# First token pair of a two-layer MLP behind attention: w_out's product turned, one float32 quad, cheaper sign handling

## The chip, the cores and the metric

One NeuronCore of a Trainium2 chip runs the whole program. Its engines are TensorE (PE in the profile, with its weight loads listed as PEld), VectorE (DVE), ScalarE (ACT), GpSimd (POOL) and SyncE (SP), whose queue issues the DMAs. The metric is the device time of one execution in microseconds; lower is better.

## The reference

Linear attention over 4 batches, 8 heads, 576 positions, head size 64, then two MLPs over 2,304 tokens with d_model 512 and d_ff 2,048. The activations are float32; the MLP weights arrive as float64.

```python
q_s = softmax(q, axis=-1); k_s = softmax(k, axis=2)
kv = np.einsum('bhsd,bhse->bhde', k_s, v)
attn = np.einsum('bhsd,bhde->bhse', q_s, kv)          # -> x [2304, 512]
h = x @ w_in;  g = maximum(h, 0) + log1p(exp(-abs(h)));  x = g @ w_out       # layer 0, softplus
h = x @ w_in2; g = where(h > 0, h, exp(minimum(h, 0)) - 1); out = g @ w_out2 # layer 1, ELU
```

## The kernel before

**Tiling.** The 2,304 tokens are six blocks of 384, taken in three pairs p = 0, 1, 2. The 2,048 hidden features are eight quads f = 0 to 7 of 256. The program runs layer m = 0 over the three pairs, then layer m = 1; inside a pair, quad after quad, "up" (h = w_in^T x, hidden features on the partitions), the activation g, and "down" (w_out's product). The down product of a quad stands beside the up product of the next one.

**Up.** A quad goes up by seven products over 2 x 2 blocks instead of eight (`add_up`, L833). Each operand is split into a rounded part and a rest (fp32r), so a product is six matmuls of 384 columns. `add_forms` makes the seven forms of x for a pair (`ts` L614, `xf` L603 and L607; forms 1 and 2 need the pair's first block only), `add_w_in` the seven forms of the weights (`st` L726, `wf` L742 and L746). The results are added up in PSUM and on DVE (`s` L846, `h` L867).

**Down.** g is split into `gh` (ACT, L969) and `gl` (DVE, L973), w_out likewise into the halves of `wo` (L766, L770). In pair 0 of layer 0 a step of `add_down` (L1045) has g as the stationary operand and 512 output features as columns, so the result has tokens on the partitions. In pairs 1 and 2 of layer 0 the product is *turned* (`add_down_turned`, L1007): w_out is stationary, the 768 tokens of the pair are the columns, in a matmul of 512 and one of 256, and output features lie on the partitions. Turned results are stored feature by feature, and layer 1 loads them as they are (`add_y`); those of pair 0 are stored by tokens, loaded again and transposed on PE (`py`, L566, 24 of them) with a copy on ACT (`sx`, L577).

**Direct quads.** Quads 0 and 1 of pair 0 take another way, since the opening has little time to prepare operands: float32 matmuls on x and the unsplit weights (`add_up_direct`, L895; down at L1040). Each float32 matmul stands as two records in the trace.

**Weights.** `add_words` turns float64 to float32 by integer operations on the two 32-bit words: ACT scales the high word (L662), DVE shifts it left (L666), DVE puts the sign back by and-or (L670, SCALAR_TENSOR_TENSOR), ACT scales the low word (L676), DVE adds (L687, a custom operation; ISA in the order). There are 32 such conversions, through two `raw` buffers.

**Attention** of a block is made just ahead of its pair: key maxima (`mx`, `pt`, `m`, `pb`), exponentials, `pk` (L390) and `kvbd`; for the queries `qm`, `qd`, `qn`, `pq` (L506), `px` (L522), and the copy into `sx` (L535). Block t = 1 belongs to pair 0 as well. The exponential and softplus need different function tables in ACT, so ACT_TABLE_LOAD stands between them.

**Order.** `Plan.order` lists every step with an estimated duration, buffers and due times, and at each turn gives an engine the ready step that is latest by its due time. `PRI` (L1344) shifts the due times of the attention steps, of the first pair's weights (i0 to i7, o0 to o7) and of others. Every engine then runs its own list in order.

Of the kernel before, what the change touches and what calls it, by code (L numbers as in the profile page):

```python
# [20 lines left out]
class Plan:  # L21
# [37 lines left out]
    def order(self):  # L59
# [23 lines left out]
        seq = []  # L83
        while len(seq) < n:
# [79 lines left out]
def attention_moe_moe_kernel(  # L164
# [97 lines left out]
    direct = lambda m, p, f: (m, p) == (0, 0) and f < 2  # L262
# [372 lines left out]
    def add_words(m, s, f, ring="ti"):  # L635
# [24 lines left out]
        @step(ACT, t_act(n), w=[rk])  # L660
        def _():
            nc.scalar.activation(hi(), hi(), AF.Copy, scale=2.0**-112)  # L662
# [350 lines left out]
    def add_down(m, p, f):  # L1013

        wk = ("wo", m, "o", f) if p == direct(m, 0, f) else ("wo", m, "o", f, p)
        t0 = after_quad(m, p, f)
        if turned(m, p):
            return add_down_turned(m, p, f, wk, t0)
# [4 lines left out]
        for (i, j, r), at in zip(order, fill):  # L1023
            j, half = at_(m, p, f, i, j)
            col = at_(m, p, f, j, half)[1] * BLK + r * P
# [3 lines left out]
            whole = direct(m, p, f)  # L1029
            gk, w32 = ("g", m, p, f, i), ("w", "ti", m, "o", f)  # L1030

            @step(
                PE, 0.86 if whole else DN, w=[] if first else [ak],
                r=[gk, w32] if whole else [hk, lk, ("woh", m, f), ("wol", m, f)], hold=[] if whole else [wk],
                make=[(ak, f"acc{half}")] if first else [], due=t0 + at + 0.01, line=("acc", half, r),
            )
            def _(col=col, j=j, hk=hk, lk=lk, ak=ak, first=first, whole=whole, gk=gk, w32=w32):
                ps = new(ak) if first else T[ak]
                if whole:
                    nc.tensor.matmul(  # L1040
                        ps, T[gk][:, col : col + P], T[w32][:, j * DM : (j + 1) * DM], start=first, stop=False,
                    )
                    return
# [241 lines left out]
    def add_store(m, p):  # L1285
# [180 lines left out]
```

## Time and profile before

| | us |
|---|---|
| three timed runs, median (range) | 833.11 (832.82 to 833.67) |
| profiled execution: its own time | 833.62 |
| its span, first to last instruction | 831.9 |
| PE busy | 809.3 |
| DVE busy | 657.5 |
| ACT busy | 564.7 |

The granted TensorE clock was full (0.998 over the span). PE's busy time is the union of matmul records, whose ends are modelled and overlap the next start; the distance between two starts tells what a matmul costs in a stream. Idle time of an engine counts only where the engine that sets the end waits for it.

### The profile page before, as it was taken

The page shows a single profiled execution, that of the slowest core. Times are in us where ns is not written, and L with a number is a line of the kernel's source. Part 1 is how long each engine was busy: PE and PEld are TensorE (multiplying, and loading weights), DVE is VectorE, ACT ScalarE, POOL GpSimd, SP SyncE. Part 2 cuts the span into 40 slices and gives each one's busy share as a digit, 9 for nine tenths or more (in the row PEclk, how much of TensorE's full clock was granted, in tenths as well). Part 3 has the DMA queues.
Part 4 walks back from the last instruction along what each step waited for, and adds up shares of the span by engine and source line. Part 5 has one row for each costly group of instructions (what it writes and reads, how often), then busy time and mean ns, then how long its engine had stood idle before and what let it go on. Part 6 is the DMA issues. An engine that isn't in the chain of part 4 may idle for free.

```text
span 831.9 us, 13270 instructions
## 1 busy us (share of the span) xinstructions
PE 809.3 (97%) x5110; PEld 732.4 (88%) x5110; DVE 657.5 (79%) x1088; ACT 564.7 (68%) x889; POOL 6.1 (1%) x28
## 2 busy tenths in 40 slices
PE   5799999999999999999999999999999999999997
PEld 4455788888889999999999998898999999999997
DVE  7879999979887768777679788968468697766775
ACT  4878987876787856756657767667466675557552
POOL 2000000000000000000000000000000000000000
PEclk9999999999999999999999999999999999999999
DMA  9597786636985556576855898987687676787563
GB/s 288 155 284 234 225 283 197 196 115 206 284 263 215 181 206 236 206 253 221 321 191 218 289 371 331 328 325 242 239 311 292 234 284 222 271 278 301 202 225 147
DMA packets 75166, 205.33 MB, mean 247 GB/s; under 512 B 18784, under 2 KB 34144, under 8 KB 65632
## 3 DMA queue, kind: packets, MB, share of 16 engines
q1 hardware_dynamic: 75104, 204.49, 71.0%
q8 instruction: 40, 0.66, 0.3%
q14 instruction: 22, 0.18, 0.1%
HBM read 143.65 MB, written 60.82 MB: 246 GB/s over the span
## 4 chain that ended last, share of the span: by engine, by line
PE 82%; DVE 8%; ACT 5%; DMA 2%; issue 2%; DVEq 0%; ACTq 0%; SPq 0%
PE ub L833 21%; PE acc L1007 15%; PE acc L1045 13%; PE uc L833 11%; PE Pb L1185 8%; PE ua L833 5%; PE Pc L1185 4%; PE Pa L1185 2%; PE px L522 1%; DMA wf_i<-wfd 1%; DVE mt L346 1%; PE acc L1040 1%; PE pk L390 1%; DMA raw_i<-in_moe_w_in_dram 1%; PE pq L506 1%
## 5 line engine op out<-in xcount | busy, mean ns | idle before, releaser
L833 PE MATMUL ub<-xf,wf_i 128*128 128x384 f32 x1104 | 226.5, 339 | 1.4 <-ACT s L846 1.1
L833 PEld LDWEIGHTS ub<-xf,wf_i 128*128 128x128 f32 x1104 | 189.3, 188 | 13.4 <-ACT s L846 4.3
L846 ACT COPY s<-ub 128x384 f32<-128x384 f32 x138 | 65.8, 477 | 72.7 <-PE ub L833 71.6
L833 PE MATMUL uc<-xf,wf_i 128*128 128x384 f32 x552 | 111.8, 337 | 0.7 <-ACT g L916 0.7
L1007 PE MATMUL acc<-gh,wo_o 128*128 128x512 f32 (+1 forms) x512 | 111.7, 340 | 0.0
L1045 PE MATMUL acc<-wo_o,gh 128*128 128x512 f32 x336 | 106.7, 398 | 0.0
L833 PEld LDWEIGHTS uc<-xf,wf_i 128*128 128x128 f32 x552 | 95.1, 188 | 5.7 <-ACT g L916 1.9
L867 DVE TENSOR_TENSOR h<-uc,s 128x384 f32<-128x384 f32 x92 | 51.1, 555 | 52.6 <-PE uc L833 47.5
L1007 PEld LDWEIGHTS acc<-gh,wo_o 128*128 128x128 f32 x512 | 82.9, 188 | 7.3
L1045 PEld LDWEIGHTS acc<-wo_o,gh 128*128 128x128 f32 x336 | 61.4, 188 | 9.0 <-ACT yt L1295 0.2
L1045 PE MATMUL acc<-wo_o,gl 128*128 128x512 f32 x168 | 66.5, 396 | 0.0
L1007 PE MATMUL acc<-gl,wo_o 128*128 128x512 f32 (+1 forms) x256 | 65.5, 336 | 0.0
L973 DVE TENSOR_TENSOR gl<-g,gh 128x768 fp32r<-128x768 f32 x60 | 57.2, 953 | 8.4 <-ACT gh L969 8.3
L833 PE MATMUL ua<-xf,wf_i 128*128 128x384 f32 x276 | 56.0, 337 | 0.0
L969 ACT CAST gh<-g 128x768 fp32r<-128x768 f32 x60 | 50.2, 836 | 7.1 <-DVE g L960 6.3
L833 PEld LDWEIGHTS ua<-xf,wf_i 128*128 128x128 f32 x276 | 47.9, 188 | 1.4 <-ACT sx L535 0.3
L746 DVE TENSOR_TENSOR wf_i<-st_i,wf_i 128x1024 fp32r<-128x1024 f32 x30 | 36.7, 1222 | 15.1 <-ACT wf_i L742 15.1
L1007 PEld LDWEIGHTS acc<-gl,wo_o 128*128 128x128 f32 x256 | 39.1, 188 | 5.3
L916 ACT ACTIVATE g<-h 128x384 f32<-128x384 f32 (+1 forms) x44 | 30.2, 686 | 16.3 <-DVE h L867 16.1
L1045 PEld LDWEIGHTS acc<-wo_o,gl 128*128 128x128 f32 x168 | 31.5, 187 | 6.8
L742 ACT CAST wf_i<-r_i 128x512 fp32r<-128x512 f32 (+1 forms) x48 | 23.2, 511 | 16.5 <-PE uc L833 16.4
L742 ACT CAST wf_i<-st_i 128x1024 fp32r<-128x1024 f32 x30 | 31.4, 1048 | 1.1 <-DVE st_i L726 1.0
(282 smaller groups left out, 1429.2 us busy)
## 6 DMA issues: line engine op xcount, KB each, us to landing
wf_i<-wfd SPq DMA_DIRECT2D x16, 1792.0 KB, 8.2
ws<-wos SPq DMA_DIRECT2D x28, 1024.0 KB, 5.4
raw_i<-in_moe_w_in_dram SPq DMA_DIRECT2D x16, 1024.0 KB, 6.5
raw_o<-in_moe_w_out_dram SPq DMA_DIRECT2D x16, 1024.0 KB, 7.4
wo_o<-wod SPq DMA_DIRECT2D x14, 1024.0 KB, 5.5
wfd<-wf_i SPq DMA_DIRECT2D x8, 1792.0 KB, 7.8
r_i<-w32i SPq DMA_DIRECT2D x24, 512.0 KB, 6.0
wod<-wo_o SPq DMA_DIRECT2D x8, 1024.0 KB, 5.2
```

What stands on the lines that cost most here:

```text
L346: top = lambda o, x, y: nc.vector.tensor_tensor(o, x, y, op=ALU.max)
L742: nc.scalar.copy(view(0, lo, n, c), get())
L746: nc.vector.tensor_tensor(view(1, lo, n, c), get(), view(0, lo, n, c).bitcast(F32), op=ALU.subtract)
L833: nc.tensor.matmul(ps[:, :BLK], T[wk][:, lo : lo + P], T[xk][:, (2 * c + kc) * BLK : (2 * c + kc + 1) * BLK], start=(i in first and kc == ...
L846: nc.scalar.copy(new(sk), T[key][:, :BLK])
L867: nc.vector.tensor_tensor(T[hk][:, half * BLK : (half + 1) * BLK], T[key][:, :BLK], T[sk], op=ALU.add)
L916: nc.scalar.activation(o, i, AF.Softplus)
L969: nc.scalar.copy(new(hk), T[gk])
L973: nc.vector.tensor_tensor(new(lk), T[gk], T[hk].bitcast(F32), op=ALU.subtract)
L1007: nc.tensor.matmul(ps, T[wk][:, lo : lo + P], T[g][:, cols], start=(first and n == 0 and starts), stop=(f == NQ - 1 and j == 1 and n == 2) ...
L1045: nc.tensor.matmul(ps, T[g][:, col : col + P], T[wk][:, (2 * a + j) * DM : (2 * a + j + 1) * DM], start=(first and n == 0), stop=(f == NQ ...
L1185: nc.tensor.matmul(ps[:, x * 256 : x * 256 + 256], T[fk][a][:, r * P : (r + 1) * P], T[ck][:, q * 512 + b * 256 : q * 512 + b * 256 + 256] ...
```

## The change

Four edits, and new numbers in `PRI`. (1) `direct` holds for quad 0 alone; quad 1 of pair 0 goes by seven products and split operands like quads 2 to 7. (2) `turned` holds for all pairs of layer 0, so pair 0 is stored by features, and layer 1 loads it without transposes. (3) Quad 0's down product is turned too, by a new function with float32 matmuls: block 0 as 384 columns, block 1 as 128 and 256. (4) Where the planner has exp's table loaded at the scaling of a high word, ACT scales by a Prelu in place of a copy: for negative numbers its slope -2^32 clears the sign and sets a bit that the shift by three moves into the sign's place, so the and-or is left out. Six of the 32 conversions go this way, five of them in pair 0, both of quad 0 among these.

```diff
+            if i in self.either and table == "exp":
+                gone.add(self.either[i][0])
+                self.light.add(self.either[i][1])
...
-    direct = lambda m, p, f: (m, p) == (0, 0) and f < 2
+    direct = lambda m, p, f: (m, p) == (0, 0) and f < 1
...
+            if tk in plan.light:
+                nc.scalar.activation(hi(), hi(), AF.Prelu, scale=2.0**-112, alpha=-(2.0**32))
+            else:
+                nc.scalar.activation(hi(), hi(), AF.Copy, scale=2.0**-112)
...
-            nc.vector.scalar_tensor_tensor(
-                T[tk], words(1), 0x80000000, T[tk], op0=ALU.bitwise_and, op1=ALU.bitwise_or
-            )
+            if tk not in plan.light:
+                nc.vector.scalar_tensor_tensor(
+                    T[tk], words(1), 0x80000000, T[tk], op0=ALU.bitwise_and, op1=ALU.bitwise_or
+                )
...
-    turned = lambda m, p: m == 0 and p > 0
+    turned = lambda m, p: m == 0
+
+    def add_down_direct(f):
...
+        for n, (t, j, kc) in enumerate((t, j, kc) for t in range(2) for j in range(2) for kc in range(KC)):
...
+                lhs = T[w32][:, j * DM + kc * P : j * DM + kc * P + P]
+                g = T[gk][:, j * BLK : (j + 1) * BLK]
+                ps = T[keys[0]]
+                if not t:
+                    nc.tensor.matmul(ps[:, :BLK], lhs, g, start=first, stop=False, skip_group_check=True)
+                    return
+                more = T[keys[1]][:, kc % 2 * 256 : kc % 2 * 256 + 256]
+                nc.tensor.matmul(ps[:, BLK:], lhs, g[:, :P], start=False, stop=False, skip_group_check=True)
+                nc.tensor.matmul(more, lhs, g[:, P:], start=first and kc % 2 == 0, stop=False, skip_group_check=True)
...
-        k00=97, q00=38, k01=54, q01=13, k02=167, q02=154, k03=94, q03=54, k10=9, q10=83, k12=24, q12=11,
...
+        k00=52.5, q00=663.5, k01=151, q01=397.5, k02=204, q02=426, k03=1516, q03=209.5, k10=55, q10=109, k12=155.5,
```

Lines move by up to 32: L607 is now L613, L614 L620, L670 L682, L687 L701, L833 L847, L895 L909, L973 L987, L1007 L1046; the new direct down product is L1014 to L1018.

DVE, the first conversion (of quad 0's w_in, `raw_i` to `w_ti_i`). Before:

```order
L666 TENSOR_SCALAR ti_i_509<-raw_i_404 128x1024
L403 RECIPROCAL rs_2_507<-rs_2_507 128x2
L491 TENSOR_TENSOR qn_2_518<-q_2_387,qd_2_500 128x2x3x64 x2
L670 SCALAR_TENSOR_TENSOR ti_i_509<-raw_i_404,ti_i_509 128x1024
L687 ISA w_ti_i_545<-raw_i_404,ti_i_509 128x2048
L607 TENSOR_TENSOR xf_0_1_550<-sx_0_175,xf_0_1_550 128x768
```

Now:

```order
L677 TENSOR_SCALAR ti_i_488<-raw_i_344 128x1024
L477 TENSOR_REDUCE qd_0_494<-q_0_414 128x6
L352 TENSOR_TENSOR mt_0_503<-k_0_442 128x512
L352 TENSOR_TENSOR mt_0_503<-mt_0_503 128x2x128
L352 TENSOR_TENSOR mt_0_503<-mt_0_503 128x2x64
L352 TENSOR_TENSOR mx_0_507<-mt_0_503,k_0_442 128x128
L482 TENSOR_SCALAR qd_0_494<-qd_0_494 128x6
L487 RECIPROCAL qd_0_494<-qd_0_494 128x6
L497 TENSOR_TENSOR q_0_414<-q_0_414,qd_0_494 128x2x3x64
L405 TENSOR_SCALAR rs_0_548<-pk_0_518 128x1
L701 ISA w_ti_i_550<-raw_i_344,ti_i_488 128x2048
```

Between the shift and the final addition the and-or L670 is gone, and steps of the query and key chains of blocks 0 and 1 stand there.

PE, the opening, from a direct product of the pair's first block to the `px` matmuls that give block 1's x for the first four heads. Before (`up_0_0_671` and `up_0_1_703` are quad 1's):

```order
L1040 MATMUL acc_0_0_2_609<-w_ti_o_592,g_0_0_0_588 128x512
L390 MATMUL pk_0_624<-v_0_525,k_0_526 64x65 x36
L895 MATMUL up_0_0_671<-sx_0_175,w_ti_i_665 128x384 x4
L506 MATMUL pq_0_694<-ident,qn_0_676 128x128 x3
L506 MATMUL pq_1_699<-ident,qn_0_676 128x128 x3
L895 MATMUL up_0_1_703<-sx_0_175,w_ti_i_665 128x384 x4
L522 MATMUL px_0_716<-xq_0_693,kvbd_0_148 128x3x64
L522 MATMUL px_0_716<-xq_0_693,kvbd_0_152 128x3x64
```

Now (`up_0_0_585` and `up_0_1_646` are quad 0's):

```order
L909 MATMUL up_0_0_585<-sx_0_175,w_ti_i_550 128x384 x4
L396 MATMUL pk_0_598<-v_0_441,k_0_442 64x65 x36
L909 MATMUL up_0_1_646<-sx_0_175,w_ti_i_550 128x384 x4
L512 MATMUL pq_0_671<-ident,qn_0_658 128x128 x3
L512 MATMUL pq_1_676<-ident,qn_0_658 128x128 x3
L1014 MATMUL acc_0_0_682<-g_0_0_0_644,w_ti_o_635 128x384
L528 MATMUL px_0_686<-xq_0_670,kvbd_0_148 128x3x64
L528 MATMUL px_0_686<-xq_0_670,kvbd_0_152 128x3x64
L528 MATMUL px_1_689<-xq_1_675,kvbd_1_149 128x3x64
L528 MATMUL px_1_689<-xq_1_675,kvbd_1_153 128x3x64
```

Quad 1's up product and all but one of the down steps of block 0 no longer stand ahead of these `px` matmuls.

DVE, where the forms of x that need both blocks begin (`ts_0_1`). Before:

```order
L670 SCALAR_TENSOR_TENSOR ti_o_689<-raw_o_611,ti_o_689 128x1024
L687 ISA w_ti_o_709<-raw_o_611,ti_o_689 128x2048
L614 TENSOR_TENSOR ts_0_1_731<-sx_1_174,sx_0_175 128x768
L666 TENSOR_SCALAR ti_i_739<-raw_i_680 128x1024
L614 TENSOR_TENSOR ts_0_2_741<-sx_1_174,ts_0_1_731 128x768
L670 SCALAR_TENSOR_TENSOR ti_i_739<-raw_i_680,ti_i_739 128x1024
L607 TENSOR_TENSOR xf_0_6_744<-ts_0_2_741,xf_0_6_744 128x768
L687 ISA ti_i_739<-raw_i_680,ti_i_739 128x2048
L607 TENSOR_TENSOR xf_0_5_754<-ts_0_1_731,xf_0_5_754 128x768
```

Now (`ti_i_663`, `st_i_0_692`, `wf_i_0_697` are quad 1's w_in):

```order
L740 TENSOR_TENSOR st_i_0_692<-st_i_0_692,ti_i_663 128x256
L760 TENSOR_TENSOR wf_i_0_697<-ti_i_663,wf_i_0_697 128x512
L740 TENSOR_TENSOR st_i_0_692<-ti_i_663 128x256
L760 TENSOR_TENSOR wf_i_0_697<-ti_i_663,wf_i_0_697 128x256
L740 TENSOR_TENSOR st_i_0_692<-ti_i_663,st_i_0_692 128x256
L620 TENSOR_TENSOR ts_0_1_718<-sx_1_176,sx_0_175 128x768
L677 TENSOR_SCALAR ti_o_721<-raw_o_654 128x1024
L620 TENSOR_TENSOR ts_0_2_724<-sx_1_176,ts_0_1_718 128x768
L682 SCALAR_TENSOR_TENSOR ti_o_721<-raw_o_654,ti_o_721 128x1024
L760 TENSOR_TENSOR wf_i_0_697<-st_i_0_692,wf_i_0_697 128x1024
L701 ISA ti_o_721<-raw_o_654,ti_o_721 128x2048
```

Two direct quads' conversions stood ahead of `ts_0_1`; now quad 1's forms of w_in do, and the and-or and rounding of the next weights stand between `ts_0_2` and the first form.

## Rows read from the trace of the kernel before

**Rows 1.** The page: span, busy time (sections 1 and 2).
```profile
PE 809.3 (97%) x5110; PEld 732.4 (88%) x5110; DVE 657.5 (79%) x1088; ACT 564.7 (68%) x889; POOL 6.1 (1%) x28
...
DVE  7879999979887768777679788968468697766775
```

**Rows 2.** Four stretches: us, busy us of each engine (instructions), clock, DMA, GB/s.
```profile
0.00:58.00 58.00, 43.03 (x413) 28.62 (x414) 46.31 (x105) 37.18 (x59) 5.71 (x25) 0.97 0.81 235
58.00:112.00 54.00, 53.61 (x276) 38.00 (x275) 53.56 (x81) 46.21 (x62) 0.13 (x1) 1.00 0.80 258
112.00:200.00 88.00, 87.66 (x493) 74.62 (x492) 78.98 (x121) 71.69 (x108) 0.13 (x1) 1.00 0.54 177
```

**Rows 3.** Timeline of PE: start us, us, engine, line, tiles, shape, xcount [idle before].
```profile
67.25 2.74 PE L895 MATMUL up<-sx,w_ti_i 128*128 128x384 f32 x8
69.83 1.02 PE L1040 MATMUL acc<-w_ti_o,g 128*128 128x512 f32 x2
...
109.09 0.62 PE L1045 MATMUL acc<-wo_o,gh 128*128 128x512 f32 x2
...
109.78 1.20 PE L833 MATMUL ub<-xf,wf_i 128*128 128x384 f32 x6
...
262.93 1.20 PE L833 MATMUL ub<-xf,wf_i 128*128 128x384 f32 x6
263.97 0.86 PE L1007 MATMUL acc<-gh,wo_o 128*128 128x512 f32 x4
264.67 0.51 PE L1007 MATMUL acc<-gl,wo_o 128*128 128x512 f32 x2
265.01 1.20 PE L833 MATMUL uc<-xf,wf_i 128*128 128x384 f32 x6
```

**Rows 4.** A group of PE, whole run: xcount | busy us, mean ns | idle before.
```profile
L566 PE MATMUL py<-ident,yl 128*128 128x128 f32 x24 | 3.6, 272 | 0.0
```

**Rows 5.** Groups of DVE from 57 to 190 us, by shape.
```profile
L973 DVE TENSOR_TENSOR gl<-g,gh 128x768 fp32r<-128x768 f32 x12 | 11.4, 954 | 0.3 <-ACT gh L969 0.3
L746 DVE TENSOR_TENSOR wf_i<-st_i,wf_i 128x1024 fp32r<-128x1024 f32 x8 | 9.8, 1223 | 1.7 <-ACT wf_i L742 1.7
L770 DVE TENSOR_TENSOR wo_o<-ti_o,wo_o 128x1024 fp32r<-128x1024 f32 x6 | 7.3, 1220 | 0.1
...
L670 DVE SCALAR_TENSOR_TENSOR ti_i<-raw_i,ti_i 128x1024 uint32<-128x1024 uint32 x6 | 7.3, 1210 | 0.0
L867 DVE TENSOR_TENSOR h<-uc,s 128x384 f32<-128x384 f32 x12 | 6.6, 554 | 1.2 <-PE uc L833 1.1
L726 DVE TENSOR_TENSOR st_i<-ti_i 128x256 f32<-128x256 f32 x12 | 5.0, 420 | 0.0
```

**Rows 6.** Groups of ACT, whole run, by shape.
```profile
L662 ACT ACTIVATE raw_o<-raw_o 128x1024 f32<-128x1024 f32 x16 | 18.4, 1152 | 0.4 <-DMA raw_o<-in_moe_w_out_dram 0.2
...
L916 ACT ACT_TABLE_LOAD x11 | 14.1, 1283 | 0.2
...
L381 ACT ACTIVATE k<-k 128x1152 f32<-128x1152 f32 x6 | 7.0, 1168 | 0.8 <-DVE k L373 0.7
```

**Rows 7.** Timelines of DVE, then PE, about 112 us.
```profile
111.09 1.22 DVE L746 TENSOR_TENSOR wf_i<-st_i,wf_i 128x1024 fp32r<-128x1024 f32 x1
...
112.57 1.22 PE L833 MATMUL ub<-xf,wf_i 128*128 128x384 f32 x6
```

**Rows 8.** Waits of DVE up to 60 us: us in total, times, longest.
```profile
DVE mt L346 <- DMA k<-in_k_dram: 3.7, 1, 3.7
...
DVE k L373 <- PE pb L366: 1.5, 1, 1.5
DVE qd L471 <- ACT q L467: 1.0, 1, 1.0
```

**Rows 9.** Timelines about the second block: PE, then DVE.
```profile
55.63 1.46 PE L522 MATMUL px<-xq,kvbd 128*128 128x192 f32 x8
...
57.72 0.96 DVE L614 TENSOR_TENSOR ts<-sx,sx 128x768 f32<-128x768 f32 x1 [2.60 <-ACT sx L535]
```

More of the change, by code (lines that the diff above doesn't have):

```diff
@@ L34, in __init__ @@
         self.maker, self.gives, self.place = {}, {}, {}
+        self.either, self.light = {}, set()
     def add(self, eng, dur, fn, r=(), w=(), new=(), due=None, after=0.0, behind=(), port=False, hold=(), tab=None):
@@ L82, in order @@
         lock, table = 0.0, "exp"
-        seq = []
+        seq, gone = [], set()
         while len(seq) < n:
@@ L116, in order @@
                 dur *= PE_EARLY
+            if i in gone:
+                dur = 0.0
+            if i in self.either and table == "exp":
+                gone.add(self.either[i][0])
+                self.light.add(self.either[i][1])
             table = self.tab[i] or table
@@ L661, in _ @@
         def _():
-            nc.scalar.activation(hi(), hi(), AF.Copy, scale=2.0**-112)
+            if tk in plan.light:
+                nc.scalar.activation(hi(), hi(), AF.Prelu, scale=2.0**-112, alpha=-(2.0**32))
+            else:
+                nc.scalar.activation(hi(), hi(), AF.Copy, scale=2.0**-112)
+        scaled = _
         @step(DVE, t_dve(n, True), r=[rk], make=[(tk, "ti")], line="ti")
@@ L973, in _ @@
             nc.vector.tensor_tensor(new(lk), T[gk], T[hk].bitcast(F32), op=ALU.subtract)
-    at_ = lambda m, p, f, j, half: (half, j) if direct(m, p, f) else (j, half)
-    turned = lambda m, p: m == 0 and p > 0
+    turned = lambda m, p: m == 0
+    def add_down_direct(f):
+        t0 = after_quad(0, 0, f)
+        pace = (7 * UP + 4 * R * DN) / (4 * KC)
+        for n, (t, j, kc) in enumerate((t, j, kc) for t in range(2) for j in range(2) for kc in range(KC)):
+            gk, w32 = ("g", 0, 0, f, t), ("w", "ti", 0, "o", f)
+            keys = [("acc", 0, 0, kc)] + [("acc", 0, 0, KC + kc // 2)] * t
+            first = f == 0 and j == 0
+            made = [keys[t]] if first and not (t and kc % 2) else []
+            @step(
+                PE, 0.65, w=[key for key in keys if key not in made], r=[gk, w32],
+                make=[(key, f"acc{kc // 2}") for key in made], due=t0 + n * pace + 0.01, line=("acc", kc),
+            )
+            def _(t=t, j=j, kc=kc, gk=gk, w32=w32, keys=keys, made=made, first=first):
+                for key in made:
+                    new(key)
+                lhs = T[w32][:, j * DM + kc * P : j * DM + kc * P + P]
[7 more added lines that the diff above has]
+                nc.tensor.matmul(more, lhs, g[:, P:], start=first and kc % 2 == 0, stop=False, skip_group_check=True)
     def add_down_turned(m, p, f, wk, t0):
@@ L1016, in add_down @@
         t0 = after_quad(m, p, f)
+        if direct(m, p, f):
+            return add_down_direct(f)
         if turned(m, p):
@@ L1023, in add_down, with _ @@
         for (i, j, r), at in zip(order, fill):
-            j, half = at_(m, p, f, i, j)
-            col = at_(m, p, f, j, half)[1] * BLK + r * P
+            j, half = i, j
+            col = half * BLK + r * P
             hk, lk, ak = ("gh", m, p, f, i), ("gl", m, p, f, i), ("acc", m, p, half, r)
             first = f == 0 and j == 0
-            whole = direct(m, p, f)
-            gk, w32 = ("g", m, p, f, i), ("w", "ti", m, "o", f)
             @step(
-                PE, 0.86 if whole else DN, w=[] if first else [ak],
-                r=[gk, w32] if whole else [hk, lk, ("woh", m, f), ("wol", m, f)], hold=[] if whole else [wk],
+                PE, DN, w=[] if first else [ak], r=[hk, lk, ("woh", m, f), ("wol", m, f)], hold=[wk],
                 make=[(ak, f"acc{half}")] if first else [], due=t0 + at + 0.01, line=("acc", half, r),
             )
-            def _(col=col, j=j, hk=hk, lk=lk, ak=ak, first=first, whole=whole, gk=gk, w32=w32):
+            def _(col=col, j=j, hk=hk, lk=lk, ak=ak, first=first):
                 ps = new(ak) if first else T[ak]
[L1039 to L1043, printed above, removed]
                 for n, (g, a) in enumerate(((hk, 0), (hk, 1), (lk, 0))):
```

7 lines of the change are left out of this document (4 added, 3 removed).

## The prediction

> **What bounds the kernel now.** I read the page's busy shares first. TensorE (PE) is busy 97% of the span and VectorE (DVE) 79%, but the slices of DVE show nines in the opening quarter and fours to eights behind it [rows 1]. So I cut the run by stage. Up to 58 us PE is busy 43.0 of 58 us. From 58 to 112 us PE and DVE are both full, 53.61 and 53.56 of 54 us; from 112 to 200 us PE is full and DVE has 9 us of room [rows 2]. The kernel is therefore PE's instruction stream, started late by the opening, and in the first pair of token blocks DVE keeps up only just.
>
> "Busy" overstates matmuls, because their recorded times overlap, so I price PE by start-to-start distances. Four float32 matmuls of 384 columns (eight records, two for each) go from 67.25 to 69.83 us: 0.645 us each. Six rounded (fp32r) matmuls of 384 columns go from 262.93 to 263.97: 0.174 us each. Three of 512 columns go from 109.09 to 109.78: 0.23 us each. One turned step, three of 512 and three of 256, goes from 263.97 to 265.01: 1.04 us [rows 3]. With these, and the small attention matmuls priced in the same way, PE's rows add up to 795 us of work. The remaining 37 us of the span are the start (5 us until the first matmul), the stores at the end (5 us) and 26 us in which PE is held up, some 17 of them before 50 us.
>
> **The change part by part: PE.** (a) Hidden quad 1 of the first pair goes up by seven products instead of directly. Removed: 16 float32 matmuls at 0.645 = 10.3 us. Added: 7 x 6 at 0.174 = 7.3 us. -3.0 us. (b) Its down product: removed 12 float32 matmuls of 512 columns; by columns from the row of 384, 0.645 x 512/384 = 0.86 each, 10.3 us; added eight turned steps at 1.04 = 8.3 us. -2.0 us. (c) Quad 0's direct down product is turned too: 8 of 384, 8 of 128 and 8 of 256 columns in place of 12 of 512. Both are 6,144 columns, 10.3 us. Zero. (d) Quads 2 to 7: twelve steps of three 512-column matmuls (12 x 0.69 = 8.3 us) become eight turned steps (8.3 us). Zero, though it is 12 instructions more for each quad. (e) The first pair's output now lies in DRAM with features in rows, so the 24 transposes L566 before the second layer go. They are at most their 3.6 us [rows 4]; at 0.645/2 x 128/384 = 0.108 us for a single-record matmul of 128 columns, 2.6 us; I take something between that and nothing hidden, 2.3 us. Sum: **-7.3 us of PE work**, and PE is the engine that sets the end from 58 us on, so all of it counts if PE can be fed as early as now. Nothing hides it.
>
> What speaks against (b) and (d) is the shorter matmul: each one has its own weight load, and the seven turned quads have 84 more of them. In the trace the turned step's 1.04 us is its columns at the pace of the 512-column rows (3 x 0.23 + 3 x 0.117), so the loads behind 256 columns are covered [rows 3], and I take zero. Uncovered they would cost 732.4 / 5110 = 0.143 us each [rows 1], 12.0 us, which is rival 3. The Trainium skill, "TensorE: Matmul & The Clock Gate" (LDWEIGHTS, and Back-to-back issue gap), says that a 128-column load takes about 107 ns however many rows it has, and that in a real stream of pairs the spacing is set by load and matmul together. By that rule an estimated 9 us of loads would come into the open; the trace's 1.04 us does not agree.
>
> **DVE and ScalarE (ACT) in the first pair.** Quad 1's new way adds on DVE, at the means of [rows 5] less 0.08 us by which neighbours overlap: four sums of its weights 1.35, three roundings 2.1 (1.14 for 1,024 columns, the rest by columns), three additions h 1.4, two gl 1.75, and the rounding of w_out 1.14, which so far is done in pair 1. Together 7.7 us. Removed: six and-ors (L670) of the 32, five of them in the first pair, 5 x 1.14 = 5.7 us. Net +2.0 us for DVE in a stretch where it has no room, while PE loses 5.0 us there. This is the part that can eat the gain, and I cost it by a balance.
>
> The balance: for each handover, DVE's work queued ahead of it (all rows of its order at the means of their groups) minus PE's work ahead of its use. That difference plus DVE's idle time until then is how far PE must lag. Before, the tightest handover is quad 4's rounded weights: DVE's 185 rows sum to 99.15 us, its row ends at 112.31, so DVE had idled 13.2 us; PE's work ahead is 89.2 us; the lag is 10.0 + 13.2, and PE takes these weights at 112.57, 0.26 us after they are ready [rows 7]. So the sum reproduces the trace. In the order of the changed kernel the tightest handovers are quad 3's rounded weights (80.6 - 66.2 = 14.4 us) and the key maximum of pair 1 (146.8 - 131.3 = 15.4 us). The lag at PE stays what it was if DVE idles 15.4 - 10.0 = 5.4 us less than now.
>
> Does it? Of the 13.2 us, 3.7 are the first key's load, 1.5 the wait L373 on a matmul queued behind a down product, 1.0 the wait on an exponential [rows 8], 2.6 the wait of ts L614 for the second block's x [rows 9]; the rest is short gaps. The second block's x is the key. Before, its last matmuls end at 57.1 us [rows 9], behind 34.9 us of PE work, quad 1's direct up product among it. Now 25.2 us stand ahead of them, so they end near 57.1 - 9.7 = 47.4, ACT's copies near 48, and DVE, with 42.0 us of work ahead of ts, reaches it at 42.0 + 3.7 + some 2.5 = 48.2: no wait. The matmul behind the wait of 1.5 now stands ahead of every down product. I take 8 us of idle: 3.7, 1.0, some 3.3 of short gaps. Bounds: 5.5 (hardly a gap) and 13.2 (as now). With 8, the lag is 15.4 + 8 = 23.4 against 23.2: +0.3 us.
>
> The multiplication that stands in for the and-or (a Prelu) has no row. Its bounds are a copy-with-scale of 1,024 columns, 1.15 us, and an exponential of 1,152, 1.17 us [rows 6]: the same pace, so I take 1.15 and no cost. (The Trainium skill, "ScalarE: Activation LUTs", What ACT_TABLE_LOAD costs, gives every function the same pace; for a Prelu no run here shows it yet.) ACT gains 4.8 us of work in the first pair (three copies s, casts of weights and of g) and loses four of 23 table loads, 4 x 1.28 = 5.1 us [rows 6]; it has 7.8 us of room from 58 to 112 us [rows 2], so both are hidden there; if ACT lost that room, 4.8 us would be the price.
>
> SP's queue: twelve stores and loads of 256 KB around the old transposes become six stores and two loads; they lie some 200 us after their writers and hide. At the pair's end the same six accumulators are copied out through the same two buffers. In the opening the raw weights still have two buffers, so the third raw load waits for the first conversion, as now; behind it in ACT's order stand the copies of the second block.
>
> **The sum**, against the profiled execution, 833.62 us (its span 831.9; the median of the three timed runs, 833.11, is 0.5 lower): 833.6 - 7.3 + 0.3 = **826.6 us**.
>
> **Rivals.** (1) *DVE idles as now.* The new order keeps 13.2 us of idle, because every handover is tighter: lag 15.4 + 13.2 = 28.6, 5.4 more than now; 833.6 - 7.3 + 5.4 = 831.7, no difference that a measurement shows. For it: both engines now wait for each other from 58 to 150 us, so short waits add up. Against: two named waits go. Idle of 10 to 13 us lies between and gives 828.5 to 831.4. (2) *The second block is late*, the slower side. If the third raw load lands late, ACT stands at it with the copies of the second block behind it, and ts cannot start. Every microsecond by which ts starts after 48.2 + (13.2 - 8) = 53.4 us adds to the 831.7; from 56.5 us on the kernel is slower by over 0.2% (834.8), and with ts at 57.7 as before it takes 836.0. For it: ts did start at 57.72 in the old order [rows 9]. Against: 9.7 us of PE work have gone from ahead of it. (3) *Weight loads in the open*: 833.6 - 7.3 + 12.0 = 838.3 us. For it: more and shorter matmuls in all eight quads; against: the turned steps of pairs 1 and 2 show the loads covered. (4) The change does not do what it says: excluded for the work, since the built order shows the instructions gone.
>
> **How the numbers follow.** Chance 0.66 for the forecast (822.5 to 829.5: idle 5.5 gives 824.1, and small waits elsewhere move 1.5 either way), 0.10 for 829.5 to 831.4, 0.02 for less than 822.5, 0.11 for rival 1 and its neighbourhood (831.4 to 834.8), 0.09 for rival 2, 0.02 for rival 3. The range 822.5 to 832.0 leaves out under 2 in 10. A measurement of this kernel can tell about 0.2%, 1.7 us: faster means under 831.4, slower over 834.8. So faster 0.78, same 0.11, slower 0.11.
>
> **What would show it.** In the changed profile: 24 transposes L566 gone and L1046 at 1.04 us a step; quad 0 alone in float32; ts of the first pair starting near 48 us (rival 1: near 53; rival 2: after 56); DVE full from there to some 150 us with PE's waits on DVE under 3 us in total. Wrong would be: PE waiting on gl, h or rounded weights from 50 to 150 us for 5 us or more, turned steps of the first pair longer than 1.1 us, or an unchanged time with all this in place, which would put a new wait behind 200 us, where I assumed none.

## The result, and the profile after

The changed kernel takes 825.21 us (median of seven runs, 824.13 to 829.62) against 833.29 for the kernel before beside it: ratio 0.9914, 95% interval 0.9899 to 0.9928. The forecast was 826.6, and 826.33 is what the profiled execution took. Five more runs in another comparison gave 825.79, ratio 0.9917 (0.9905 to 0.9929).

The page of the changed kernel, its busy shares and VectorE's (DVE) slices, answers to [rows 1]:

```profile
PE 803.3 (97%) x5216; PEld 744.6 (90%) x5216; DVE 656.0 (80%) x1094; ACT 559.7 (68%) x886; POOL 6.3 (1%) x28
...
DVE  7899999968988767777779688877468697767674
```

106 matmul records more, yet TensorE (PE) is busy 6 us less. The same three stretches as in [rows 2] (us, busy us of PE, its loads, DVE, ACT and POOL, clock, DMA, GB/s):

```profile
0.00:58.00 58.00, 42.88 (x411) 31.10 (x412) 48.05 (x111) 37.99 (x62) 5.57 (x25) 0.97 0.86 244
58.00:112.00 54.00, 54.00 (x302) 48.72 (x301) 53.69 (x80) 45.10 (x63) 0.00 (x0) 1.00 0.73 236
112.00:200.00 88.00, 87.64 (x617) 79.07 (x616) 79.01 (x126) 72.74 (x109) 0.56 (x2) 1.00 0.62 202
```

DVE is full from 58 to 112 us, as before, and PE now is to the last hundredth. PE's waits from 50 to 200 us shrink from four lines, 0.9 us in all, to one (waited for: us, times, longest):

```profile
PE ua L847 <- ACT kvbd L422: 0.4, 1, 0.4
```

I price PE's stream as the prediction did: every record at the pace of its shape (start to start), and what its starts are later than that I call *held up*. So "PE work" is a count of instructions times paces of the trace; that the paces hold is seen where the held-up time of a full stretch stays near zero. "Median" is that of all runs of the kernel in its comparison, "profiled" the traced execution to which the rest belongs; all in us.

| kernel | median | profiled | PE work | held up | before 50 | 50 to 150 | 150 to 250 | later |
|---|---|---|---|---|---|---|---|---|
| before | 833.3 | 833.6 | 795.95 | 25.9 | 16.7 | 1.7 | 4.1 | 3.4 |
| changed | 825.2 | 826.3 | 788.69 | 26.0 | 20.0 | 1.6 | 1.5 | 3.0 |
| after_again | 825.8 | 825.1 | 788.69 | 24.8 | 19.0 | 1.6 | 1.5 | 2.8 |
| keep_andor | 829.7 | 828.5 | 788.69 | 28.1 | 19.2 | 3.9 | 2.5 | 2.7 |
| raw_early | 823.7 | 823.2 | 788.69 | 22.9 | 16.7 | 1.6 | 1.6 | 3.1 |
| raw_early_again | 823.3 | 823.6 | 788.69 | 23.1 | 16.7 | 1.5 | 1.7 | 3.2 |
| raw_early_andor | 830.0 | 829.7 | 788.69 | 29.4 | 19.0 | 3.9 | 2.5 | 4.0 |
| double_pq | 828.1 | 825.3 | 791.28 | 22.4 | 16.7 | 1.6 | 1.5 | 2.6 |
| turn_only | 834.2 | 832.6 | 793.73 | 26.8 | 15.6 | 6.3 | 1.6 | 3.3 |
| light_only | 832.2 | 833.7 | 795.95 | 25.8 | 14.2 | 6.3 | 1.7 | 3.7 |
| two_direct | 837.2 | 838.8 | 793.73 | 33.0 | 21.0 | 4.9 | 3.2 | 3.9 |
| no_turn | 859.5 | 860.1 | 790.91 | 57.4 | 20.0 | 5.7 | 3.2 | 28.5 |
| no_turn_y | 832.2 | 834.0 | 790.91 | 31.3 | 20.1 | 5.7 | 3.2 | 2.3 |
| old_pri | 845.3 | 845.9 | 788.69 | 45.6 | 16.0 | 23.0 | 1.7 | 5.0 |

The first two rows are the answer in short: PE's work fell by 7.26 us, the held-up time stayed in its sum (25.9, 26.0) and moved within it: 3.3 us more in the opening, 2.6 less between 150 and 250 us. So the new order by itself gained nothing that the table shows; the kernel before with the new numbers alone was not run.

Quad 0 alone is left in float32, 32 records up and 16, 16 and 16 down; no transpose (L572, before L566) is in the trace:

```profile
L909 PE MATMUL up<-sx,w_ti_i 128*128 128x384 f32 x32 | 12.6, 549 | 0.8 <-ACT sx L541 0.8
L1014 PE MATMUL acc<-g,w_ti_o 128*128 128x384 f32 x16 | 6.0, 486 | 0.0
L1018 PE MATMUL acc<-g,w_ti_o 128*128 128x256 f32 x16 | 4.8, 380 | 0.0
L1017 PE MATMUL acc<-g,w_ti_o 128*128 128x128 f32 x16 | 3.1, 274 | 0.0
```

The opening is the surprise. ACT's group of the new multiplication (L669) and PE's timeline there (start, us [idle before]):

```profile
L669 ACT ACTIVATE raw_i<-raw_i 128x1024 f32<-128x1024 f32 x3 | 3.4, 1140 | 0.0
L669 ACT ACTIVATE raw_o<-raw_o 128x1024 f32<-128x1024 f32 x3 | 3.4, 1138 | 3.3 <-DMA raw_o<-in_moe_w_out_dram 3.3
```

```profile
36.71 0.91 PE L528 MATMUL px<-xq,kvbd 128*128 128x384 f32 x2 [2.14 <-ACT xq L518]
38.47 4.47 PE L909 MATMUL up<-sx,w_ti_i 128*128 128x384 f32 x8 [0.84 <-ACT sx L541]
42.87 2.32 PE L396 MATMUL pk<-v,k 64*64 64x65 f32 x72
45.12 2.85 PE L909 MATMUL up<-sx,w_ti_i 128*128 128x384 f32 x8
```

The Prelu costs 1.14 us, a copy's price. But quad 0's w_out words are late: the `raw_o` row below shows ACT standing 2.07 us for their load with the copy `xq` behind it, PE idles 2.14 us, and then eight records take 4.47 us that 7 us later take 2.85. DVE waits for the same words; below ACT's row stands the line of DVE's waits up to 60 us.

```profile
35.16 1.14 ACT L669 ACTIVATE raw_o<-raw_o 128x1024 f32<-128x1024 f32 x1 [2.07 <-DMA raw_o<-in_moe_w_out_dram]
```

```profile
DVE ti_o L677 <- ACT raw_o L669: 1.8, 1, 1.8
```

### The profile page after: what moved, and what is told of

Read it like the earlier page. It is cut to its first block, busy times and chain, and to the rows that moved or that the text cites. A ratio compares the mean times of both kernels' runs of the same rounds, so it can differ in the third digit from the quotient of the medians.

```text
span 824.5 us, 13469 instructions
## 1 busy us (share of the span) xinstructions
PE 803.3 (97%) x5216; PEld 744.6 (90%) x5216; DVE 656.0 (80%) x1094; ACT 559.7 (68%) x886; POOL 6.3 (1%) x28
## 4 chain that ended last, share of the span: by engine, by line
PE 91%; ACT 3%; DMA 2%; DVE 2%; issue 1%; SPq 0%; DVEq 0%
PE ub L847 23%; PE acc L1046 21%; PE uc L847 11%; PE Pb L1217 8%; PE acc L1077 8%; PE ua L847 6%; PE Pc L1217 4%; PE Pa L1217 2%; PE pk L396 2%; PE up L909 2%; PE px L528 1%; DMA raw_o<-in_moe_w_out_dram 1%; PE pq L512 1%; PE acc L1014 1%; DMA k<-in_k_dram 1%
## 5 line engine op out<-in xcount | busy, mean ns | idle before, releaser
L847 PE MATMUL ub<-xf,wf_i 128*128 128x384 f32 x1128 | 229.9, 338 | 0.9 <-ACT s L860 0.8
L847 PEld LDWEIGHTS ub<-xf,wf_i 128*128 128x128 f32 x1128 | 192.3, 188 | 10.0 <-ACT s L860 2.2
L1046 PE MATMUL acc<-gh,wo_o 128*128 128x512 f32 x736 | 161.4, 341 | 0.0
L1046 PEld LDWEIGHTS acc<-gh,wo_o 128*128 128x128 f32 x736 | 119.0, 188 | 12.1 <-issue 0.5
L847 PE MATMUL uc<-xf,wf_i 128*128 128x384 f32 x564 | 114.7, 338 | 0.0
L847 PEld LDWEIGHTS uc<-xf,wf_i 128*128 128x128 f32 x564 | 96.5, 188 | 3.7 <-DVE h L881 0.2
L1046 PE MATMUL acc<-gl,wo_o 128*128 128x512 f32 x368 | 94.0, 336 | 0.0
L987 DVE TENSOR_TENSOR gl<-g,gh 128x768 fp32r<-128x768 f32 x62 | 59.1, 953 | 18.7 <-ACT gh L983 18.6
L1046 PEld LDWEIGHTS acc<-gl,wo_o 128*128 128x128 f32 x368 | 56.2, 188 | 7.7
L1077 PE MATMUL acc<-wo_o,gh 128*128 128x512 f32 x192 | 59.7, 392 | 0.0
L847 PE MATMUL ua<-xf,wf_i 128*128 128x384 f32 x282 | 57.0, 336 | 0.4 <-ACT kvbd L422 0.4
L847 PEld LDWEIGHTS ua<-xf,wf_i 128*128 128x128 f32 x282 | 48.8, 188 | 1.4 <-ACT kvbd L422 0.7
L1077 PEld LDWEIGHTS acc<-wo_o,gh 128*128 128x128 f32 x192 | 35.4, 188 | 4.4
L1077 PE MATMUL acc<-wo_o,gl 128*128 128x512 f32 x96 | 38.0, 396 | 0.0
L866 ACT COPY h<-ub 128x384 f32<-128x384 f32 x24 | 11.5, 480 | 26.6 <-PE ub L847 26.3
```

The source lines that it names most:

```text
L847: nc.tensor.matmul(ps[:, :BLK], T[wk][:, lo : lo + P], T[xk][:, (2 * c + kc) * BLK : (2 * c + kc + 1) * BLK], start=(i in first and kc == ...
L987: nc.vector.tensor_tensor(new(lk), T[gk], T[hk].bitcast(F32), op=ALU.subtract)
L1046: nc.tensor.matmul(ps, T[wk][:, lo : lo + P], T[g][:, cols], start=(first and n == 0 and starts), stop=(f == NQ - 1 and j == 1 and n == 2) ...
L1077: nc.tensor.matmul(ps, T[g][:, col : col + P], T[wk][:, (2 * a + j) * DM : (2 * a + j + 1) * DM], start=(first and n == 0), stop=(f == NQ ...
```

## The experiments

**Theory:** the gain is PE work, 5.0 us from quad 1's way and 2.3 from the transposes; DVE's queue, 15.4 us of work ahead of PE's plus its idle time, is just short of holding PE up. (A handover is a place where PE needs what DVE made; it is the tighter, the more of DVE's work stands ahead of it than of PE's.) **Rivals:** the new order's better feeding is the gain; or the and-or's removal; or one part is nothing and another all.

**after_again**, the changed kernel itself. 

> The changed kernel itself, once more, as the measure for the runs beside it. Theory (the gain is TensorE work taken away, 7.3 us, and the feeding of TensorE costs what it did): 825 to 826 us, some 7.5 us below the kernel before. Rival (part of the 8 us came from a favourable opening in that one comparison): above 827 us.

Measured: 825.79 us (825.14 to 827.32). The result stands; its traced opening holds PE up 1 us less than the first trace's.

### The transposes and the turned product

**turn_only**, the kernel before with pair 0 turned (edits 2 and 3 of the change; the new direct down product serves both direct quads; one line of the edit):

```diff
-    turned = lambda m, p: m == 0 and p > 0
+    turned = lambda m, p: m == 0
...
```

> The kernel before with one part of the change: pair 0 of layer 0 is turned, both direct quads among it (their down product by float32 matmuls of 384, 128 and 256 columns); two direct quads, all and-ors and the old order's numbers stay. Theory: the 24 transposes go and nothing else changes in TensorE's work, -2.3 us (between -3.6 and 0), 830.8 us. Rival A (the loads behind the 256-column matmuls of quads 2 to 7 come into the open): slower than before, up to 843 us. Rival B (the whole gain of the change is the turning): 825 to 826 us.

Measured: 834.21 us, ratio 1.0016 (1.0005 to 1.0026): 1.2 us *slower*. Both the theory's 830.8 and rival B's 825 are refuted as times. In the trace PE's work is 2.22 us less, and 4.6 us are held up anew between 50 and 150 us; the opening gives 1.1 of them back, and the stretch from 150 to 250 us another 2.5. DVE's first waits from 50 to 60 us show what is late:

```profile
DVE ti_i L677 <- ACT raw_i L671: 3.5, 1, 3.5
DVE w_ti_o L700 <- ACT raw_o L689: 0.7, 1, 0.7
```

The planner put the steps in another order, and DVE stands 3.5 us for the next quad's words. The traced execution, at 832.6, was the fastest of the twelve; its granted clock over the span was 1.0, that of the others 0.994 to 0.999, so up to 4 us of the others' time is not in a trace. Rival A's 843 didn't come: a turned step of the changed kernel's first pair still takes 154.97 - 153.93 = 1.04 us, as in [rows 3]:

```profile
153.93 0.86 PE L1046 MATMUL acc<-gh,wo_o 128*128 128x512 f32 x4
154.62 0.51 PE L1046 MATMUL acc<-gl,wo_o 128*128 128x512 f32 x2
154.97 0.86 PE L1046 MATMUL acc<-gh,wo_o 128*128 128x512 f32 x4
```

**no_turn**, the changed kernel without turning pair 0, quad 0's direct down product as it was before (one line of the edit):

```diff
-    turned = lambda m, p: m == 0
+    turned = lambda m, p: m == 0 and p > 0
...
```

> The changed kernel with pair 0 of layer 0 left unturned: tokens on the partitions, stores by tokens, 24 transposes before layer 1, quad 0's direct down product as before; one direct quad, the multiplication for the and-or, and the new order's numbers stay. Theory: the transposes' 2.3 us come back, and the planner's order for this shape has a looser handover (18.7 instead of 15.4 us of VectorE's work ahead of TensorE's), 18.7 + 10.7 us of idle = 29.4 against the 27.0 that TensorE lags in the changed kernel, so 827.5 without and 829.9 us with that. Rival A (the transposes were hidden or free): 825.2 us. Rival B (the shorter matmuls of the seven turned quads cost something by their weight loads, so that turning took away less than it gave): below 825 us.

Measured: 859.52 us, far outside every theory. Most of it (25.5 us of held-up time between 450 and 500 us) lies at the border of the layers, where PE waits for the loads of pair 0's stored output, its transposes and the forms made from them. The waits that its trace names there come to 14.2 us; the rest is in good part matmuls at the lower clock, the granted clock of the stretch being 0.74. One stretch of this kernel, then of the next (columns as in [rows 2]):

```profile
440.00:500.00 60.00, 45.73 (x209) 38.93 (x209) 34.88 (x56) 29.70 (x47) 0.00 (x0) 0.74 0.64 228
```

```profile
440.00:500.00 60.00, 60.00 (x325) 55.00 (x325) 51.14 (x83) 43.04 (x67) 0.00 (x0) 1.00 0.83 297
```

**no_turn_y** is no_turn with two of the planner's numbers put back:

```diff
-        y=-20.5, ahead=6.5,
+        y=59, ahead=148,
```

> The run no_turn again with the old numbers for the stores and loads between the layers (y = 59, ahead = 148 in place of -20.5 and 6.5), since the new ones were made for a kernel without transposes and that run stood still for some 25 us at the layers' border (between 450 and 500 us). Theory: the border's stall goes; what is left are 2.3 us of transposes and a looser handover in the first pair (18.7 us + 9.8 of idle = 28.5 against TensorE's lag of 25.7 us there): 828 to 831 us. Rival (transposes cost nothing where TensorE is fed): 825.8 us, or 828.6 with the looser handover.

Measured: 832.16 us (831.04 to 836.22), ratio 0.9991 (0.9978 to 1.0004). The border's stall is gone, so it was the order's and not the transposes' price. PE's work is 2.22 us above the changed kernel's, as the theory says, but the time is 1.2 us past its range. The other 4 us are hold-ups: in the trace, an execution 1.8 us above the median, 8.9 us lie between 50 and 250 us, against 3.1 in the changed kernel, more than the 2.8 that the handover was to cost. What the transposes cost in time is therefore not told by this run.

**double_pq** prices 24 transposes in an unchanged order:

```diff
-                for r in range(R):
+                for r in [r for r in range(R) for _ in range(2 if t > 3 else 1)]:
                     nc.tensor.transpose(
```

> The changed kernel in the same order with 24 transposes more on TensorE: those that turn pair 2's normalised queries (L512, identity matrix as one operand, 128 columns, float32: the shape of the 24 that the change took away) are done twice, between 200 and 320 us, where TensorE is full. It is the price of 24 such transposes by itself, with no other part of the change touched. Theory: 24 x 0.108 = 2.6 us, nothing hides them, 828.4 us (2.2 to 3.6 us, 828.0 to 829.4). Rival (single transposes among long matmuls cost nothing): 825.8 us.

Measured: 828.12 us, ratio 0.9948 (0.9934 to 0.9961), +2.3 us on after_again: the theory's 2.6 within its error, and not the rival's zero. Its six runs spread from 825.31 to 830.46; the fastest is the traced one, and its opening (16.7 us held up, no wait of ACT for the w_out words) is that of raw_early below. Beside raw_early's trace, with the same opening, it takes 825.31 - 823.20 = 2.1 us more.

### Quad 1

**two_direct**, the changed kernel with quad 1 direct again:

```diff
-    direct = lambda m, p, f: (m, p) == (0, 0) and f < 1
+    direct = lambda m, p, f: (m, p) == (0, 0) and f < 2
```

> The changed kernel with quad 1 direct again (float32 matmuls up and down, its down product turned like quad 0's); turning, the multiplication for the and-or and the new numbers stay. Theory: TensorE's work is 5.0 us more (the terms (a) and (b) of the prediction), VectorE's is some 7 us less, so the handovers behind the opening are loose, and TensorE's hold-ups stay at what its late start makes them: 825.8 + 5.0 = 830.8 us (829.5 to 832). Rival (the float32 quad was cheap because it filled time in which TensorE waited anyway): 825 to 827 us.

Measured: 837.15 us, ratio 1.0059 (1.0047 to 1.0071). The work is 5.04 us more, the theory's term to the tenth; the rival is refuted. But 8.2 us more are held up than in after_again, where the theory had none. The longest stop behind the opening is this one, PE's for ACT's copy `xq`:

```profile
PE pq L512 <- ACT xq L518: 1.9, 1, 1.9
```

ACT is busy 19.79 of the 20 us up to 140 us (in the changed kernel 16.64), and PE's stop begins at 139 us; my balance counted DVE's queue and not ACT's. Two of the three loads of a function table that stand in ACT's list there are shown below the stretch; this kernel has 25 of them, the changed one 19. The stretch, columns as in [rows 2], then ACT's rows:

```profile
120.00:140.00 20.00, 19.21 (x169) 17.26 (x167) 18.28 (x32) 19.79 (x27) 0.13 (x1) 1.00 0.95 319
```

```profile
129.08 1.28 ACT L473 ACT_TABLE_LOAD   x1
136.55 1.28 ACT L930 ACT_TABLE_LOAD   x1
```

This stop is 1.9 of the 8.2 us; the opening has 2.0, and the rest is spread over later, shorter ones.

### The and-or

**keep_andor**, the changed kernel in the same order with the and-or on DVE:

```diff
-            if tk in plan.light:
+            if False:
...
-            if tk not in plan.light:
+            if True:
```

> The changed kernel in the same order, but every high word is scaled by a copy and gets its and-or on VectorE, so VectorE has six instructions of 1.14 us more, five of them in the first pair, and TensorE's and ScalarE's work is what it was. Theory (VectorE and TensorE hand over to each other without slack up to the key maximum of pair 1's second block, which was ready at 157.94 us and used at 158.32): 5.7 us less 0.4 us of slack, less up to 2.3 us that the two and-ors of the opening can hide in VectorE's waits there: +3.0 to +5.3 us at that place, 828 to 830.5 us if it stays. Rival A (VectorE's relief bought nothing, since TensorE's work alone sets the time): 825.2 +- 1 us. Rival B (a later lag takes it in, since TensorE is held up for another 1.8 us between 160 and 300 us anyway): 826.4 to 828.7 us.

Measured: 829.66 us (828.54 to 832.14), ratio 0.9964 (0.9951 to 0.9976): +3.9 us on after_again, within the theory's 3.0 to 5.3; rival A's 825 and rival B's upper end of 828.7 are passed. It is held up where DVE is full; PE's waits from 50 to 300 us, against one line in the changed kernel:

```profile
PE ua L847 <- ACT kvbd L422: 1.5, 1, 1.5
PE pq L512 <- ACT g L930: 0.8, 1, 0.8
PE ub L847 <- ACT s L860: 0.8, 1, 0.8
```

They name ACT, which stands for DVE: at `g`, behind a cast of `ti_i`, for 1.87 us (0.61 in the changed kernel), and at `kvbd`, behind a cast of `ti_o`, for 1.59 us (0.50). Both words come from DVE behind an and-or, and the second stand, for which the trace names no releaser, ends 0.08 us after DVE's addition for `ti_o` does. ACT's rows:

```profile
100.00 0.92 ACT L756 CAST wf_i<-ti_i 128x512 fp32r<-128x512 f32 x2 [1.87 <-DVE ti_i L701]
129.17 1.05 ACT L780 CAST wo_o<-ti_o 128x1024 fp32r<-128x1024 f32 x1 [1.59 <-issue]
```

The key maximum of pair 1's second block ends on DVE at 160.47 us; in the changed kernel at 157.94:

```profile
160.19 0.28 DVE L364 TENSOR_REDUCE m<-pt 128x2 f32<-128x128 f32 x1
```

**light_only**, the kernel before with the multiplication alone (nine conversions in its order; the edit is the change's `either` and `light` lines). 

> The kernel before with one part of the change: the multiplication in place of the and-or where exp's table is in (nine conversions of 32 in this order); both direct quads, the transposes and the old numbers stay. Theory: TensorE's work is what it was; only the 6 us by which it is held up between 50 and 300 us could shrink, and the opening sets most of TensorE's lag: -0.5 us (between -2 and +1), 832.5 us. Rival (VectorE's relief is a good part of the gain by itself): -4 us or more, 829 us or less.

Measured: 832.19 us, ratio 0.9984 (0.9976 to 0.9993): -0.8 us. The theory's -0.5 holds. Held up before 50 us: 2.5 us less; between 50 and 150: 4.6 more; between 150 and 250: 2.4 less. So taking nine and-ors out is worth under 1 us in this order, where quad 1 is direct, and taking six out 3.9 us in the changed one, where it isn't. That they pay for the seven-product quad is a guess from this: the two kernels differ in their orders too.

### The order

**old_pri**, the changed kernel with the old numbers in `PRI`:

```diff
-        k00=52.5, q00=663.5, k01=151, q01=397.5, k02=204, q02=426, k03=1516, q03=209.5, k10=55, q10=109, k12=155.5,
+        k00=97, q00=38, k01=54, q01=13, k02=167, q02=154, k03=94, q03=54, k10=9, q10=83, k12=24, q12=11,
...
```

> The changed kernel with the old numbers in PRI: the same instructions but for the planner's order (and the conversions that it finds under exp's table). TensorE's work is 7.3 us less than before, as in the changed kernel. Theory (the feeding in the first pair decides how much of that shows): in this order the tightest handover is the second rest of quad 1's g, 24.2 us of VectorE's work ahead of TensorE's, not 15.4; with 8 to 12 us of idle that is a lag of 32 to 36 us against the 25.7 of the changed kernel: +6.5 to +10.5, 832 to 836 us, no gain over the kernel before or a loss. Rival (TensorE's work is the gain whatever the order): 826 us.

Measured: 845.25 us, ratio 1.0139 (1.0124 to 1.0153). The rival is refuted, the theory's sign is right, and its 832 to 836 is too low by 9 us. 23 us are held up between 50 and 150 us. PE's first two waits from 50 to 110 us:

```profile
PE ub L847 <- ACT s L860: 4.8, 2, 4.1
PE uc L847 <- DVE h L881: 3.3, 1, 3.3
```

All waits that the trace names from 50 to 150 us come to 13.3 us, so some 10 of the 23 are something else. The granted clock from 50 to 95 us is 0.81, and matmuls behind the waits run at the lower level: eight records of the same product take 4.53 us and, 5 us later, 2.85. My 832 to 836 counted the lag alone and not this.

```profile
60.34 4.53 PE L909 MATMUL up<-sx,w_ti_i 128*128 128x384 f32 x8
65.45 2.85 PE L909 MATMUL up<-sx,w_ti_i 128*128 128x384 f32 x8 [0.58 <-ACT g L930]
```

### The opening's load

**raw_early**, one load moved ahead by one place in SyncE's (SP's) queue:

```diff
-        return [self.steps[i][2] for _, _, i in sorted(seq)]
+        seq = [i for _, _, i in sorted(seq)]
+        loads = [i for i in seq if self.steps[i][0] == DMA]
+        ahead = loads[loads.index(self.first_o) - 1]
+        seq.remove(self.first_o)
+        seq.insert(seq.index(ahead), self.first_o)
+        return [self.steps[i][2] for i in seq]
...
```

> The changed kernel with one load moved in SyncE's queue: quad 0's w_out words are loaded ahead of the second block's first keys instead of behind them. In the changed kernel the keys' load stands 8.2 us for a buffer that TensorE's products read, and the words behind it land so late that ScalarE waits 2.1 us for them with the copies of the first block behind it; TensorE idles from 34.6 to 36.7 us, and its granted clock is 0.56 to 0.59 from 38 to 42 us. Nothing else is moved. Theory (what holds TensorE back later is the larger of its own late start and VectorE's balance, 15.4 us plus VectorE's idle): TensorE starts up to 3.7 us earlier, VectorE idles 1.8 us less, 15.4 + 8.9 = 24.3 us of lag in place of 27.0: -2.7 us, 822.5 us, and the granted clock stays full at 38 to 42 us. Rival A (the later pairs need the lag that the opening makes, so that every microsecond comes back as a later wait): 825.2 us with TensorE's waits moved to 150 to 300 us. Rival B (TensorE's late start alone sets it): -3.7 us, 821.5 us.

Measured: 823.74 us (823.20 to 825.14), ratio 0.9891 (0.9878 to 0.9904): 2.05 us below after_again, the best kernel of this study. The load's issue on SP in the changed kernel, then in raw_early:

```profile
25.17 0.43 SPq L657 DMA_DIRECT2D raw_o<-in_moe_w_out_dram  x1
```

```profile
15.89 0.43 SPq L662 DMA_DIRECT2D raw_o<-in_moe_w_out_dram  x1
```

ACT's use of the words no longer waits, and quad 0's up product starts 2.7 us earlier at full pace:

```profile
32.40 1.17 ACT L677 ACTIVATE raw_o<-raw_o 128x1024 f32<-128x1024 f32 x1
```

```profile
35.77 2.85 PE L917 MATMUL up<-sx,w_ti_i 128*128 128x384 f32 x8 [0.77 <-ACT sx L546]
```

Of the 2.3 us that the opening gives (16.7 against 19.0) 1.9 are still there at the end (held up 22.9 against 24.8): rival A, which had them come back later, is refuted. DVE's key maximum ends at 154.56 us and not 157.94; 1.8 of these 3.4 us are DVE's own wait for the same words, which is gone. So both engines moved together. -2.05 and, below, -2.46 us lie nearer to the theory's -2.7 than to rival B's -3.7; but both sums started from the first trace's opening, which is 1 us longer than after_again's, so the two are not told apart by more than that.

**raw_early_again**, the same. 

> raw_early once more. In the traces with the changed kernel's queue order ScalarE waits between 0 and 2.5 us for quad 0's w_out words, by how long that load takes, and the changed kernel's times spread from 824.1 to 829.6 us. Theory (the load's landing is what moves the changed kernel's late start from run to run, and loading it earlier takes the wait out for good): a median of 823.2 to 824.2 us, 1.5 to 2.5 below the changed kernel, no wait of ScalarE for that load, and times that lie within 2.5 us of each other. Rival (the first four runs of it were lucky): a median above 825 us or a spread like the changed kernel's.

Measured: 823.33 us (823.16 to 823.58), ratio 0.9884 (0.9867 to 0.9900). In its trace ACT doesn't wait for that load either; the eight runs of both comparisons lie within 2 us, where the changed kernel's twelve span 5.5.

**raw_early_andor** (keep_andor's and raw_early's edits together). 

> keep_andor (all and-ors on VectorE) and raw_early (the one load moved forward) together. Theory (the lag of TensorE is the larger of two: its own late start, and VectorE's balance): with the and-ors VectorE's balance binds, 21.1 us plus the 7.5 us that VectorE idled in keep_andor, and the earlier load takes at most 1 us of that idle; so of raw_early's 2.05 us next to nothing shows: 828.7 to 829.7 us. Rival (the two add up, each has its own price): 829.66 - 2.05 = 827.6 us.

Measured: 829.99 us, ratio 0.9962 (0.9950 to 0.9974), what keep_andor takes: the two do not add up. With the and-ors DVE is the longer queue (its key maximum ends at 160.22 us, in keep_andor at 160.47). PE's first product of quad 0 starts at 36.60 us and not 37.94, but that is waited away before 50 us: held up until then 19.0 against 19.2.

## Why the prediction was right, and where it was not

*PE's work, -7.3 us: right.* The priced stream fell by 7.26. Turning is 2.22 of it (turn_only, no_turn_y), quad 1 is 5.04 (two_direct). The paces hold: 1.04 us for a turned step, 0.65 for quad 0's float32 matmul, and 24 transposes cost +2.3 us when they are put in by themselves (double_pq). Rival 3 fell with the turned step: its 84 more weight loads stayed covered. (The Trainium skill, "TensorE: Matmul & The Clock Gate", Back-to-back issue gap, has load and matmul set the spacing together; for these operands the 1.04 us does not agree.)

*The feeding, +0.3 us: the sum right by luck, the terms wrong.* I had `ts` start near 48 us; it starts at 52.73, straight behind DVE's own row:

```profile
52.39 0.42 DVE L740 TENSOR_TENSOR st_i<-ti_i,st_i 128x256 f32<-128x256 f32 x1
52.73 0.95 DVE L620 TENSOR_TENSOR ts<-sx,sx 128x768 f32<-128x768 f32 x1
```

"No wait" was right, the time was not: 52.73 us is the sign that the prediction had written down for rival 1 (near 53). DVE's idle time ahead of the key maximum was put at 8 us; its row ends at 157.94 with 146.75 us of work, so it was 11.2. The step that failed is "in the opening the raw weights still have two buffers, so the third raw load waits ... as now": I looked at the third load, and it was the second, quad 0's w_out, that came late. It has a free buffer (raw_early, with the same two, loads it at 15.89 us) and stands in SP's queue behind a key load, which waits 8.2 us for PE, by the queue's waits in the changed kernel:

```profile
SPq L315 <- PE pk L396: 8.2, 1, 8.2
```

It is rival 2's mechanism, a raw load with copies behind it in ACT's order, in the first block and not the second. In the changed kernel it costs 2 us (raw_early).

By my own balance 11.2 us of idle gives a lag of 15.4 + 11.2 = 26.6 against 23.2, so 829.7 us and not 826.3; the prediction itself had said 828.5 to 831.4 for an idle of 10 to 13 us. The other half of the error is on the side of the kernel before: I took its lag as constant behind 112 us, and its trace holds PE up for another 4.1 us between 150 and 250 us, the changed kernel's for 1.5. Two mis-sized terms of some 3 us cancelled, and that the forecast came within half a microsecond is luck. Why the old order loses those 2.6 us is open: its trace names waits for `g`, `h` and `s` of 1.3 us in all there, no run was made for it, and turn_only and light_only, with the old numbers, don't lose them.

*DVE and the and-or: right.* The forecast called DVE's balance the part that can eat the gain. keep_andor shows that the six and-ors would have eaten 3.9 us of it, and old_pri that an order with a worse handover (24.2 us of DVE's work ahead of PE's, by the balance, in place of 15.4) eats all of it and 12 us more. The key maximum, which the balance named among the tightest handovers, is ready at 157.94 us and used 0.38 us later in the changed kernel; DVE's row, then PE's:

```profile
157.66 0.28 DVE L364 TENSOR_REDUCE m<-pt 128x2 f32<-128x128 f32 x1
```

```profile
158.32 0.44 PE L372 MATMUL pb<-ident,m 128*64 128x128 f32 x4
```

*ACT: right.* The Prelu is 1.14 us for the 1.15 taken, the table loads went from 23 to 19, and PE's only wait on ACT from 50 to 200 us is 0.4 us.

*Which part is worth what in time* can't be read off the partial kernels: turn_only, two_direct and no_turn_y each bring an order of the planner's own, and hold PE up by 0.9 to 8.2 us more than their neighbours. What is shown is the work of each part and that the order decides how much of it is seen.

## What to carry to other kernels

Price the engine that sets the end by start-to-start distances, and keep its work and its hold-ups in separate columns: the priced work came out within 0.1 us of its forecast in every kernel here, and every miss was a hold-up. A long wait of PE can cost twice, once by itself and once by the lower clock behind it (4.47 us in place of 2.85 for eight records here). When an edit moves work to a second engine that is full in that stage, remove something from it in the same edit, and count both queues up to each handover, ACT's too. Look in the DMA queue for a load that has a free buffer but stands behind one that waits: moving it one place was worth 2 us here.

## What the runs showed of the hardware

*TensorE's clock is low behind the opening's gaps.* In the changed kernel PE is idle for 2.14 and 0.84 us with one short product between, and the granted clock of the next four us is 0.57, so mostly the lower of its two levels (1.2 of 2.4 GHz); in raw_early, without the long gap, it is 1.00. (raw_early's clock is lower earlier, 0.87 from 20 to 30 us; in raw_early_again it is 1.00 there and from 38 to 42 us, and the time is the same.) The same stretch in both (columns as in [rows 2]):

```profile
38.00:42.00 4.00, 3.53 (x6) 2.04 (x7) 4.00 (x4) 3.92 (x7) 0.00 (x0) 0.57 0.90 309
```

```profile
38.00:42.00 4.00, 4.00 (x78) 2.99 (x78) 3.95 (x8) 3.97 (x6) 0.13 (x1) 1.00 0.75 295
```

It cost 4.47 - 2.85 = 1.62 us on eight matmul records, nearly as much as the wait itself.

*The same load takes a different time in each execution.* With the queue order unchanged, quad 0's w_out words, issued between 23.9 and 25.2 us, took 10.0 us from issue to landing in the changed kernel's trace, 9.0 in after_again's, 10.2 in keep_andor's and 7.7 in double_pq's. ACT's wait for them was 2.1, 1.3, 0.2 and nothing; in keep_andor ACT itself came later. That goes with the spread of those kernels' times, and the spread is gone where the load is issued 9 us earlier; that it is the whole cause is not shown.
